# Writing the recurrence's output transposed, in two column halves, and packing it into features by SBUF transfers

## The chip, the cores and the metric

The kernel runs on one core of a Trainium2 chip. The metric is the device time in microseconds. The kernel before takes 729.41 us, the median of three runs (729.29 to 730.01). A profile of one execution, with every instruction's start and duration, is what the readings below come from.

## What is computed

A gated recurrence (4 batches, 8 heads, 768 tokens, head dimension 48), and a SwiGLU MLP (384 to 1536 to 384) on its output, with the heads side by side as 384 features of 3072 tokens:

```python
f = 1.0 / (1.0 + np.exp(-f_logit))
for t in range(S):
    state = f[:, :, t, :, None] * state + np.einsum('bhd,bhe->bhde', k[:, :, t], v[:, :, t])
    y[:, :, t] = np.einsum('bhd,bhde->bhe', q[:, :, t], state)
x = y.transpose(0, 2, 1, 3).reshape(B * S, H * D)
g = x @ w_gate
out = (g * (1.0 / (1.0 + np.exp(-g))) * (x @ w_val)) @ w_out
```

All data is float32 on the chip (the weights come as 64-bit floats and are converted there).

## The kernel before, in words

`short_path` does the work; `general_path` is a fallback that a flag selects at the end and that these inputs do not take. The tokens are cut into 6 chunks `c` of 128. A unit is one batch `b` of one chunk, so a chunk has 4 units and there are 24. The 8 heads form 4 pairs `a`; the two heads of a pair (`par` 0 and 1) lie in partition halves that begin at 0 and 64, each using 48 rows (`rows_of`, L448).

`attention(u)` (L454) is a generator that yields between steps. Step 0 transposes the gate logits of a unit on TensorE (`fTp`, L462) and applies the sigmoid on ScalarE (L467). Step 1 makes products of gates by a scan on VectorE (L472). Step 2 transposes `k` and `q` (L462), scales them (L483 to L487) and, after the first chunk, asks for the loads of the unit three ahead (`load_after`, L489) and decays the state on GpSimd (L491). Step 3 makes the scores `sc` (L499: the two heads of a pair use the two row halves of the array), masks them to `A` on VectorE (L501) and transposes `k` back (`kt`, L506). Step 4 makes the output `y` (L516 and L519), copies it to `x` (L522), and updates the state through `dS` (L526), whose heads alternate between two partition halves of the output. Step 5 transposes `x` into features by tokens (`xTp`, L542) and copies it into the chunk's `xT` (L543), which holds all 4 units, 512 tokens.

In L516 and L519 the tokens are the stationary operand (`qT` and `A`, 128 columns) and the state (96 columns for a pair) or `v` (48 columns for a head) streams, so `y` comes out with tokens in partitions.

`mlp(c)` (L558) is a list of pieces: 24 that make the hidden layer (`gate` and `val`, 12 of each, L564, each 3 matmuls over 512 tokens), then 4 `down` (L577), one for each batch, 12 matmuls each (L580), followed by a copy and a store on ScalarE's queue (L583, L585). Every `gate` and `val` streams the whole `xT` of the chunk, so the first `gate` needs all 4 units.

The order of work is set in three places. First, chunk 0's attention is written out by hand with `run(b, steps)` (L628 to L660), and `in_order` ties TensorE, VectorE and ScalarE to it, not the SP queue. Second, `mlp(c)` and the attention of chunk c+1 take turns (`take_turns`, L590): `attention_steps` (L550) groups the steps of each unit by `parts = [1, 2, 1, 1, 1]` and sorts those groups by `2 * b + s`, and step group i of n falls due after a proportional number of MLP pieces. In chunk 0 the MLP's pieces also include the calls that fetch and convert weights (`weights`, L602). Third, the framework orders each engine's and each queue's instructions by its own plan of readiness, with program order as the priority, so something that is ready earlier can pass what is not.

All loads of q, k, v and f (`load`, L378) and of weights (L399) are issued on the SP queue; only the stores of the output go through ScalarE's queue. There are 3 buffers for each of `f`, `k` and `q`, 6 for `v`, 2 for `xT` and for `x`, 4 PSUM banks for the attention (`bank`, L451) and 4 for the MLP.

Of the kernel before, what the change touches and what calls it, by code (L numbers as in the profile page):

```python
# [9 lines left out]
FP32 = mybir.dt.float32  # L10
# [279 lines left out]
def short_path(ctx, tc, least, judge, q, k, v, f_logit, moe_w_gate, moe_w_val, moe_w_out, out):  # L290
# [9 lines left out]
    nc = tc.nc  # L300
    B, H, S, D = q.shape
    C = 128
    NCH = S // C
    HP = H // 2
    W = 64
    DM = H * D
    KT = DM // 128
    DFF = moe_w_out.shape[0]
    NF = DFF // 128
    TB = B * C  # L310
# [6 lines left out]
    att = ctx.enter_context(tc.tile_pool(name="att", bufs=2))  # L317
    ffn = ctx.enter_context(tc.tile_pool(name="ffn", bufs=2))
# [5 lines left out]
    ident = const.tile([128, 128], FP32, tag="ident", name="ident")  # L324
# [12 lines left out]
    def keep_warm(n):  # L337
        p = fps.tile([128, 512], FP32, tag="m", name="idle")
        for _ in range(n):
            nc.tensor.matmul(p, lhsT=blank[:, 0:128], rhs=blank, start=True, stop=True)  # L340
# [15 lines left out]
    def pairs(t, off=0):  # L356
        return t[:, off:off + HP * N1].rearrange("p (a t) -> p a t", t=N1)
# [18 lines left out]
    vt = {}  # L376
# [69 lines left out]
    xT = {}  # L446

    def rows_of(par):  # L448
        return slice(W * par, W * par + D)

    def bank(name):  # L451
        return aps.tile([128, 512], FP32, tag="a", name=name)

    def attention(u):  # L454
        b, c = units[u]
        fr, kr, qr = (raw[nm][u % NRAW] for nm in "fkq")
        gate, tail, start = (x[u % NROT] for x in (gates, tails, starts))

        def transposed(name, src):
            p = bank(name)  # L460
            for a in range(HP):
                nc.tensor.transpose(p[:, a * C:(a + 1) * C],  # L462
                                    src[:, 2 * a:2 * a + 2, :].rearrange("t r d -> t (r d)"), ident)
            return p.rearrange("p (a t) -> p a t", t=C)

        p = transposed("fTp", fr)
        nc.scalar.activation(pairs(gate)[:, :, 1:N1], p, AF.Sigmoid)  # L467
        yield


        n = HP * N1
        nc.vector.tensor_tensor_scan(tail[:, 0:n][:, ::-1], gate[:, 0:n][:, ::-1], ones[:, ::-1], 1.0,  # L472
                                     op0=ALU.mult, op1=ALU.add)
        whole = pairs(tail)[:, :, 1:2]
        nc.vector.tensor_tensor(least, least, whole.rearrange("p a t -> p (a t)"), ALU.min)
        nc.vector.tensor_single_scalar(pairs(start)[:, :, 0:1], whole, LEAST, op=ALU.max)
        nc.vector.reciprocal(pairs(start)[:, :, 0:1], pairs(start)[:, :, 0:1])
        yield

        kp = transposed("kTp", kr)  # L480
        qp = transposed("qTp", qr)
        kT = att.tile([128, HP, C], FP32, tag="kT", name="kT")
        nc.vector.tensor_tensor(kT, kp, pairs(tail, 2)[:, :, 0:C], ALU.mult)  # L483
        head = att.tile([128, n], FP32, tag="head", name="head", bufs=1)
        nc.vector.tensor_tensor_scan(head, gate[:, 0:n], start, 1.0, op0=ALU.mult, op1=ALU.add)  # L485
        qT = att.tile([128, HP, C], FP32, tag="qT", name="qT")
        nc.vector.tensor_tensor(qT, qp, pairs(head)[:, :, 1:N1], ALU.mult)  # L487
        if c:
            load_after(u)  # L489
            decayed = att.tile([128, HP, 2, D], FP32, tag="decayed", name="decayed")  # L490
            nc.gpsimd.tensor_tensor(decayed, states[b], whole.unsqueeze(2).broadcast_to((128, HP, 2, D)), ALU.mult)  # L491
        yield

        A = att.tile([128, 2, HP, C], FP32, tag="A", name="A")
        sc = [bank("sc") for _ in range(2)]
        for a in range(HP):
            for par in range(2):
                r = rows_of(par)
                nc.tensor.matmul(sc[par][:, a * C:(a + 1) * C], lhsT=kT[r, a, :], rhs=qT[r, a, :], start=True, stop=True)  # L499
        for par in range(2):  # L500
            nc.vector.tensor_tensor(A[:, par], sc[par].rearrange("p (a t) -> p a t", t=C),  # L501
                                    causal.unsqueeze(1).broadcast_to((128, HP, C)), ALU.mult)
        if c < NCH - 1:
            p = bank("kt")
            for a in range(HP):
                nc.tensor.transpose(p[:, a * C:(a + 1) * C], kT[:, a, :], ident)  # L506
            kt = att.tile([128, H, W], FP32, tag="kt", name="kt")
            nc.scalar.copy(kt, p.rearrange("t (h d) -> t h d", d=W))
        yield


        y = bank("y")
        for a in range(HP):
            both = y[:, 2 * a * D:2 * (a + 1) * D]
            if c:
                nc.tensor.matmul(both, lhsT=qT[:, a, :], rhs=decayed[:, a, :, :].rearrange("p r d -> p (r d)"),  # L516
                                 start=True, stop=False, skip_group_check=True)
            for par in range(2):
                nc.tensor.matmul(both[:, par * D:(par + 1) * D], lhsT=A[:, par, a, :], rhs=vt[u][:, 2 * a + par, :],  # L519
                                 start=(c == 0), stop=True, skip_group_check=True)  # L520
        x = att.tile([128, DM], FP32, tag="x", name="x")
        nc.scalar.copy(x, y[:, 0:DM])  # L522
        if c < NCH - 1:
            p = bank("dS")
            for h in range(H):
                nc.tensor.matmul(p[W * (h % 2):W * (h % 2) + W, (h // 2) * D:(h // 2 + 1) * D],  # L526
                                 lhsT=kt[:, h, :], rhs=vt[u][:, h, :], start=True, stop=True)
            dS = p[:, 0:HP * D].rearrange("p (a d) -> p a d", d=D)
            for par in range(2):
                half = slice(W * par, W * par + W)  # L530
                if c:
                    nc.vector.tensor_tensor(states[b][half, :, par, :], decayed[half, :, par, :], dS[half], ALU.add)  # L532
                else:
                    nc.scalar.copy(states[b][half, :, par, :], dS[half])
        yield


        if b == 0:
            xT[c] = ffn.tile([128, KT, TB], FP32, tag="xT", name="xT", bufs=2)
        p = bank("xTp")  # L540
        for i in range(KT):
            nc.tensor.transpose(p[:, i * C:(i + 1) * C], x[:, i * 128:(i + 1) * 128], ident)  # L542
        nc.scalar.copy(xT[c][:, :, b * C:(b + 1) * C], p[:, 0:KT * C].rearrange("p (a t) -> p a t", t=C))  # L543
        yield

    def load_after(u):
        if u + NRAW < len(units):
            load(u + NRAW)

    def attention_steps(c):  # L550

        runs = [attention(c * B + b) for b in range(B)]
        parts = [1, 2, 1, 1, 1]
        order = sorted((2 * b + s, b, n) for b in range(B) for s, n in enumerate(parts))
        return [lambda b=b, n=n: [next(runs[b]) for _ in range(n)] for _, b, n in order]

# [57 lines left out]
    mark = traced[-1]  # L614
    keep_warm(5)
    first = [attention(b) for b in range(B)]
    done = [0] * B

# [9 lines left out]
    def run(b, *steps):  # L628
        for s in steps:
            assert done[b] == s  # L630
            done[b] += 1
            next(first[b])
# [5 lines left out]
    for b in range(1, B):  # L638
        if b == 1:
            run(1, 0)  # L640
            keep_warm(12)
        run(b, 1)
        run(b - 1, 3)
        run(b, 2)
        if b + 1 < B:
            run(b + 1, 0)
        else:
            sizes.pop(0)()
        run(b - 1, 4)
        if b > 1:  # L650
            run(b - 2, 5)
            load_after(b - 1)
    run(B - 1, 3)
    joins.pop(0)()
    run(B - 1, 4)
    run(B - 2, 5)
    run(B - 1, 5)
    sizes.pop(0)()
    joins.pop(0)()
    load_after(B - 1)  # L660
# [3 lines left out]
    for c in range(NCH):  # L664
        pieces = mlp(c)
        if c == 0:
            hidden, pieces = pieces[:2 * NF], pieces[2 * NF:]
            turns = [1] * NF
            for i in range(len(joins) - NF):
                turns[NF - 1 - i] += 1  # L670
            pieces = [f for i in range(NF) for f in hidden[2 * i:2 * i + 2] + [weights] * turns[i]] + pieces
        take_turns(pieces, attention_steps(c + 1) if c + 1 < NCH else [])
        if c == NCH - 2:
            judge(bank)
# [4 lines left out]
def kernel(  # L679
# [22 lines left out]
    def judge(bank):  # L702
# [9 lines left out]
                                   skip_runtime_bounds_check_because="a comparison"))  # L712

    short_path(tc, least, judge, *args)
    with tc.If(redo[0] > 0):
        general_path(tc, *args)
# [32 lines left out]
```

## Time and profile before

| | us |
|---|---|
| three runs, median | 729.41 |
| the profiled execution | 729.66 |
| its span, first to last instruction | 727.9 |
| mean granted TensorE clock | 0.998 of full speed |

Groups that the change touches, from the groups of instructions (busy time is summed over overlapping instructions):

| group | instructions | busy us | mean ns |
|---|---|---|---|
| `y` from state, L516, TensorE | 160 | 32.8 | 286 |
| `y` from `A`, L519, TensorE | 384 | 53.5 | 267 |
| `xTp`, L542, TensorE | 72 | 11.8 | 275 |
| copy `x`, L522, ScalarE | 24 | 11.5 | 478 |
| copy `xT`, L543, ScalarE | 24 | 11.4 | 479 |

The duration of a matmul in these rows includes its passage through the array; matmuls overlap, so what one costs is read from the distance between starts. An f32 matmul appears as two instructions, a transpose as one. In a timeline line the first number is the start in us from the span's beginning, the second the time that the merged instructions cover, then engine, line, operation, output and inputs, count, and in brackets idle time before it with what ended it. SPq and ACTq are the issue of transfers by those queues.

### The profile page before, as it was taken

The page shows a single profiled execution, that of the slowest core. Times are in us where ns is not written, and L with a number is a line of the kernel's source. Part 1 is how long each engine was busy: PE and PEld are TensorE (multiplying, and loading weights), DVE is VectorE, ACT ScalarE, POOL GpSimd, SP SyncE. Part 2 cuts the span into 40 slices and gives each one's busy share as a digit, 9 for nine tenths or more (in the row PEclk, how much of TensorE's full clock was granted, in tenths as well). Part 3 has the DMA queues.
Part 4 walks back from the last instruction along what each step waited for, and adds up shares of the span by engine and source line. Part 5 has one row for each costly group of instructions (what it writes and reads, how often), then busy time and mean ns, then how long its engine had stood idle before and what let it go on. Part 6 is the DMA issues. An engine that isn't in the chain of part 4 may idle for free.

```text
span 727.9 us, 7635 instructions
## 1 busy us (share of the span) xinstructions
PE 718.8 (99%) x3146; PEld 415.8 (57%) x3146; DVE 248.9 (34%) x405; ACT 185.2 (25%) x272; POOL 21.6 (3%) x43
## 2 busy tenths in 40 slices
PE   8999999999999999999999999999999999999997
PEld 6845555655555665555566555556555566544454
DVE  8799797024234003333202433311333320011100
ACT  2655473032212103323103213301223210100100
POOL 2000000000000000000000000000000000000000
PEclk9999999999999999999999999999999999999999
DMA  9988463112111002211101112010200000000000
GB/s 194 249 224 226 140 172 76 32 35 43 32 33 40 26 23 44 44 23 32 33 23 43 33 33 43 12 32 23 45 1 1 0 1 23 23 0 1 0 23 24
DMA packets 109772, 38.34 MB, mean 53 GB/s; under 512 B 100512, under 2 KB 103584, under 8 KB 109728
## 3 DMA queue, kind: packets, MB, share of 16 engines
q1 hardware_dynamic: 106272, 33.04, 19.5%
q10 hardware_dynamic: 3456, 4.72, 1.8%
q8 instruction: 27, 0.44, 0.2%
q14 instruction: 17, 0.14, 0.1%
HBM read 33.03 MB, written 4.72 MB: 52 GB/s over the span
## 4 chain that ended last, share of the span: by engine, by line
PE 97%; DVE 1%; ACT 1%; DMA 1%; SPq 0%; issue 0%; DVEq 0%
PE o L580 26%; PE val L564 26%; PE gate L564 26%; PE y L519 5%; PE sc L499 4%; PE y L516 3%; PE dS L526 2%; PE kt L506 2%; PE qTp L462 1%; PE kTp L462 1%; PE fTp L462 1%; PE xTp L542 1%; DMA fraw<-in_f_logit_dram 1%; PE idle L340 0%; ACT xT L543 0%; ACT ob L583 0%
## 5 line engine op out<-in xcount | busy, mean ns | idle before, releaser
L564 PE MATMUL gate<-xT,w_gate 128*128 128x512 f32 x432 | 196.4, 596 | 0.8 <-ACT xT L543 0.5
L564 PE MATMUL val<-xT,w_val 128*128 128x512 f32 x432 | 195.7, 595 | 0.1
L580 PE MATMUL o<-w_out,h 128*128 128x384 f32 x576 | 188.8, 487 | 0.0
L580 PEld LDWEIGHTS o<-w_out,h 128*128 128x128 f32 x576 | 108.3, 190 | 73.2 <-issue 0.5
L564 PEld LDWEIGHTS val<-xT,w_val 128*128 128x128 f32 x432 | 79.1, 190 | 86.5 <-issue 84.9
L564 PEld LDWEIGHTS gate<-xT,w_gate 128*128 128x128 f32 x432 | 78.5, 190 | 84.4 <-issue 81.8
L575 DVE TENSOR_TENSOR h<-h,val 128x512 f32<-128x512 f32 x72 | 49.2, 684 | 184.0 <-PE val L564 184.0
L571 ACT ACTIVATE h<-gate 128x512 f32<-128x512 f32 x72 | 42.9, 597 | 205.6 <-PE gate L564 205.4
L472 DVE TENSOR_TENSOR_SCAN tails<-gates,ones 128x516 f32<-128x516 f32 x24 | 29.5, 1231 | 91.5 <-ACT gates L467 91.5
L501 DVE TENSOR_TENSOR A<-sc,causal 128x512 f32<-128x512 f32 x48 | 30.9, 684 | 81.2 <-PE sc L499 81.2
L583 ACT COPY ob<-o 128x384 f32<-128x384 f32 x24 | 11.5, 478 | 183.5 <-PE o L580 183.5
L519 PE MATMUL y<-v,A 128*128 128x48 f32 x384 | 53.5, 267 | 0.4 <-issue 0.2
L519 PEld LDWEIGHTS y<-v,A 128*128 128x128 f32 x384 | 49.7, 192 | 0.8 <-issue 0.4
L491 POOL TENSOR_TENSOR decayed<-state,tails 128x384 f32<-128x384 f32 x20 | 17.4, 868 | 561.8 <-DVE tails L472 561.8
L485 DVE TENSOR_TENSOR_SCAN head<-gates,starts 128x516 f32<-128x516 f32 x24 | 33.4, 1391 | 0.6
L516 PE MATMUL y<-decayed,qT 128*128 128x96 f32 x160 | 32.8, 286 | 0.0
L499 PEld LDWEIGHTS sc<-qT,kT 48*128 48x128 f32 x384 | 23.6, 187 | 15.3 <-issue 13.6
L516 PEld LDWEIGHTS y<-decayed,qT 128*128 128x128 f32 x160 | 25.8, 192 | 8.5 <-issue 6.9
L467 ACT ACT_TABLE_LOAD x20 | 25.7, 1283 | 16.1 <-PE fTp L462 13.5
L499 PE MATMUL sc<-qT,kT 48*128 48x128 f32 x384 | 28.4, 285 | 0.0
L532 DVE TENSOR_TENSOR state<-decayed,dS 64x192 f32<-64x192 f32 x32 | 11.2, 351 | 48.2 <-PE dS L526 47.9
L571 ACT ACT_TABLE_LOAD x20 | 25.7, 1283 | 0.4
(58 smaller groups left out, 350.3 us busy)
## 6 DMA issues: line engine op xcount, KB each, us to landing
fraw<-in_f_logit_dram SPq DMA_DIRECT2D x24, 192.0 KB, 3.1
kraw<-in_k_dram SPq DMA_DIRECT2D x24, 192.0 KB, 3.0
qraw<-in_q_dram SPq DMA_DIRECT2D x24, 192.0 KB, 3.5
v<-in_v_dram SPq DMA_DIRECT2D x24, 192.0 KB, 3.5
w<-in_moe_w_gate_dram SPq DMA_DIRECT2D x6, 768.0 KB, 6.2
w<-in_moe_w_val_dram SPq DMA_DIRECT2D x6, 768.0 KB, 5.9
w<-in_moe_w_out_dram SPq DMA_DIRECT2D x6, 768.0 KB, 4.4
out_dram<-ob ACTq DMA_DIRECT2D x24, 192.0 KB, 1.8
```

The source lines that it names most:

```text
L462: nc.tensor.transpose(p[:, a * C:(a + 1) * C], src[:, 2 * a:2 * a + 2, :].rearrange("t r d -> t (r d)"), ident)
L467: nc.scalar.activation(pairs(gate)[:, :, 1:N1], p, AF.Sigmoid)
L472: nc.vector.tensor_tensor_scan(tail[:, 0:n][:, ::-1], gate[:, 0:n][:, ::-1], ones[:, ::-1], 1.0, op0=ALU.mult, op1=ALU.add)
L485: nc.vector.tensor_tensor_scan(head, gate[:, 0:n], start, 1.0, op0=ALU.mult, op1=ALU.add)
L499: nc.tensor.matmul(sc[par][:, a * C:(a + 1) * C], lhsT=kT[r, a, :], rhs=qT[r, a, :], start=True, stop=True)
L501: nc.vector.tensor_tensor(A[:, par], sc[par].rearrange("p (a t) -> p a t", t=C), causal.unsqueeze(1).broadcast_to((128, HP, C)), ALU.mult)
L516: nc.tensor.matmul(both, lhsT=qT[:, a, :], rhs=decayed[:, a, :, :].rearrange("p r d -> p (r d)"), start=True, stop=False, skip_group_check ...
L519: nc.tensor.matmul(both[:, par * D:(par + 1) * D], lhsT=A[:, par, a, :], rhs=vt[u][:, 2 * a + par, :], start=(c == 0), stop=True, skip_gro ...
L564: nc.tensor.matmul(p, lhsT=w[:, i, j * 128:(j + 1) * 128], rhs=xT[c][:, i, :], start=(i == 0), stop=(i == KT - 1))
L571: nc.scalar.activation(h[j], p, AF.Silu)
L575: nc.vector.tensor_tensor(h[j], h[j], p, ALU.mult)
L580: nc.tensor.matmul(p, lhsT=h[j][:, b * C:(b + 1) * C], rhs=w_out[:, j, :], start=(j == 0), stop=(j == NF - 1))
```

## The change

`y` is written with features in partitions: `v` (48 columns for a head) and the decayed state (48 columns for a head) are now loaded, and the tokens (`A` and `qT`, 128 columns) stream. The heads of a pair write two partition halves of one PSUM bank (0 to 47 and 64 to 111), and pair `a` writes columns 128a to 128a+127. Two ScalarE copies, one for each half, bring it to `x`. Then transfers issued on the SP queue move rows of `x` to the rows of `xT` at which their features belong: one transfer for a head, two for a head whose 48 features cross a multiple of 128 (heads 2 and 5), 10 for each unit. The transpose step is gone, so `parts` has one entry less and the hand-written start has no step 5.

```diff
+        if b == 0:
+            xT[c] = ffn.tile([128, KT, TB], FP32, tag="xT", name="xT", bufs=2)
         y = bank("y")
         for a in range(HP):
-            both = y[:, 2 * a * D:2 * (a + 1) * D]
+            cols = slice(a * C, (a + 1) * C)
             if c:
-                nc.tensor.matmul(both, lhsT=qT[:, a, :], rhs=decayed[:, a, :, :].rearrange("p r d -> p (r d)"),
-                                 start=True, stop=False, skip_group_check=True)
+                for par in range(2):
+                    nc.tensor.matmul(y[rows_of(par), cols], lhsT=decayed[:, a, par, :], rhs=qT[:, a, :],
+                                     start=True, stop=False, skip_group_check=True)
             for par in range(2):
-                nc.tensor.matmul(both[:, par * D:(par + 1) * D], lhsT=A[:, par, a, :], rhs=vt[u][:, 2 * a + par, :],
+                nc.tensor.matmul(y[rows_of(par), cols], lhsT=vt[u][:, 2 * a + par, :], rhs=A[:, par, a, :],
                                  start=(c == 0), stop=True, skip_group_check=True)
-        x = att.tile([128, DM], FP32, tag="x", name="x")
-        nc.scalar.copy(x, y[:, 0:DM])
+        x = att.tile([128, HP, C], FP32, tag="x", name="x")
+        for par in range(2):
+            nc.scalar.copy(x[rows_of(par)], y[rows_of(par)].rearrange("p (a t) -> p a t", t=C))
+
+        for h in range(H):
+            f = h * D
+            while f < (h + 1) * D:
+                n = min((h + 1) * D, (f // 128 + 1) * 128) - f
+                r = W * (h % 2) + f - h * D
+                nc.sync.dma_start(out=xT[c][f % 128:f % 128 + n, f // 128, b * C:(b + 1) * C],
+                                  in_=x[r:r + n, h // 2, :])
+                f += n
...
-        if b == 0:
-            xT[c] = ffn.tile([128, KT, TB], FP32, tag="xT", name="xT", bufs=2)
-        p = bank("xTp")
-        for i in range(KT):
-            nc.tensor.transpose(p[:, i * C:(i + 1) * C], x[:, i * 128:(i + 1) * 128], ident)
-        nc.scalar.copy(xT[c][:, :, b * C:(b + 1) * C], p[:, 0:KT * C].rearrange("p (a t) -> p a t", t=C))
-        yield
...
-        parts = [1, 2, 1, 1, 1]
+        parts = [1, 2, 1, 1]
...
         if b > 1:
-            run(b - 2, 5)
             load_after(b - 1)
...
     run(B - 1, 4)
-    run(B - 2, 5)
-    run(B - 1, 5)
```

## The prediction

> **What bounds the kernel now.** I read the busy shares first, then the slices, then the chain that ended last.
>
> ```profile
> PE 718.8 (99%) x3146; PEld 415.8 (57%) x3146; DVE 248.9 (34%) x405; ACT 185.2 (25%) x272; POOL 21.6 (3%) x43
> ...
> PE   8999999999999999999999999999999999999997
> ...
> DMA  9988463112111002211101112010200000000000
> ...
> PE 97%; DVE 1%; ACT 1%; DMA 1%; SPq 0%; issue 0%; DVEq 0%
> ```
>
> TensorE is the chain nearly everywhere: time removed there is gained and every hole made there is paid. Only in the first two slices (36 us) are the DMA engines and VectorE full as well. A timeline of one steady unit shows what its matmuls cost, and one of the last chunk boundary what stands between a chunk's last `y` and the next MLP's first `gate`:
>
> ```profile
> 167.97 1.16 PE L499 MATMUL sc<-qT,kT 48*128 48x128 f32 x16
> ...
> 177.09 0.43 PE L516 MATMUL y<-decayed,qT 128*128 128x96 f32 x2
> ...
> 177.35 0.57 PE L519 MATMUL y<-v,A 128*128 128x48 f32 x4
> 177.85 0.55 PEld L526 LDWEIGHTS dS<-v,kt 128*64 128x64 f32 x16
> 177.85 0.67 PE L526 MATMUL dS<-v,kt 128*64 128x48 f32 x16
> 177.96 0.48 ACT L522 COPY x<-y 128x384 f32<-128x384 f32 x1 [3.12 <-PE y L519]
> ```
>
> ```profile
> 620.48 0.57 PE L519 MATMUL y<-v,A 128*128 128x48 f32 x4
> ...
> 620.88 7.97 PE L580 MATMUL o<-w_out,h 128*128 128x384 f32 x24
> ...
> 628.69 0.49 PE L542 MATMUL xTp<-ident,x 128*128 128x128 f32 x3
> ...
> 629.27 0.48 ACT L543 COPY xT<-xTp 128x384 f32<-128x384 f32 x1
> ...
> 629.80 2.41 PE L564 MATMUL gate<-xT,w_gate 128*128 128x512 f32 x5 [0.51 <-ACT xT L543]
> ```
>
> See in the first: an f32 matmul is two instructions; six of them (two of L516, four of L519) take 0.67 us, 112 ns each, although they stream only 96 or 48 columns. `dS`, whose outputs alternate between partition halves 0 and 64, does 16 in 0.60 us. In the second: the last unit's `y` is followed by a whole `down` (7.9 us) before its transpose, so `gate` waits only 0.8 us.
>
> **What the skill says.** "TensorE: Matmul & The Clock Gate", section "LDWEIGHTS", prices a weight load at columns / 1.2 ns: 107 ns for 128 columns, 40 for 48. The trace agrees: `y` paced at 112 by loads of 128 columns. The same page, "Part 3: Packing small matmuls — row/col tiling", says that matmuls in different column groups run together. The trace agrees: single records of `dS` start in pairs 6 ns apart, a pair each 58 ns; those of `sc` (row halves, 128 columns streamed) a pair each 112 ns. "TensorEngine Tiling (Array Packing)", "Key Properties", says that a change of tiling mode drains the array: from the last `y` record to the first `dS` is 205 ns instead of 112, some 0.09 us for the change.
>
> **The change, part by part.**
>
> *Matmuls of `y`.* Now, chunks 1 to 5: first `y` record to first `dS` 2.70 us per unit; in chunk 0 (no state term) 1.81. Then: per pair `a`, two state and two `A` matmuls of two instructions, 8, so 32 per unit, halves alternating. Streaming 128 columns as `sc` does, with 48-column loads underneath, gives 16 pairs x 0.112 = 1.79 us; chunk 0, 8 pairs, 0.90. The mode change moves ahead of `y` (+0.09); chunk 5, with no `dS` to share it, pays both ends (+0.19). Saved: 0.82 per unit in chunks 1 to 4, 0.63 in chunk 5, 0.82 in chunk 0. No row shows full rows with 128 columns in two column halves. The bounds are 1.79 (the halves run together) and 32 x 0.112 = 3.58 (they don't). I take 1.79, as `dS` shows halves with all rows.
>
> *Transposes `xTp`.* Three instructions, 187.16 to 187.48: 0.33 us per unit gone from TensorE.
>
> TensorE sum: 16 x 1.15 + 4 x 0.96 = **-22.2 us** in chunks 1 to 5. Chunk 0's four units would give 4.6, but there VectorE sets the pace (units 5.4 us apart, its scans, products and masks near 6 us per unit), and what follows waits on transfers anyway: I count 0.
>
> *ScalarE.* Before, two copies of 0.48. Then two copies of 512 columns each (the `kt` copy of that width took 0.59): 1.2 us in a row, before the first half-1 head can be sent.
>
> *The packing.* Per unit 10 transfers on SP (heads 2 and 5 cross a border of 128 features), 240 in all, each behind the `x` copies, and `gate` behind all of them. Prices:
>
> ```profile
> 162.48 0.37 SPq L382 DMA_DIRECT2D kraw<-in_k_dram  x1
> ...
> 162.94 0.53 SPq L382 DMA_DIRECT2D qraw<-in_q_dram  x1
> ```
>
> ```profile
> fraw<-in_f_logit_dram SPq DMA_DIRECT2D x24, 192.0 KB, 3.1
> ...
> out_dram<-ob ACTq DMA_DIRECT2D x24, 192.0 KB, 1.8
> ```
>
> Two issues in a row start 0.46 us apart; a landing takes 1.8 to 3.1 us. No row shows an SBUF to SBUF transfer of 24 KB. "DMA: Bandwidth & Descriptors", "Anatomy of one DMA", gives about 2 us fixed; I take 1.8, the store's row (bounds 1.4 and 3.1). From the end of `y`: copies 1.25, nine issues after the second copy (the last begins at 1.35 + 8 x 0.44 = 4.9), landing 6.7, with one load among them about **7 us** (bounds 5.8 and 9). For the first three units of a chunk it is hidden: many microseconds of MLP lie behind. For the fourth it is not, because its cover goes too. With `parts` of four steps a chunk has 16 steps over 28 MLP pieces, and the last step falls due after piece 28, the last `down`; before, with 20 steps, `y` of unit 3 fell after piece 27 and only the transpose after 28. The trace follows these positions (`y` between the last two `down`s), so now all of `down` comes ahead of the last `y`, and nothing but the next attention is left to hide the packing.
>
> *Boundaries into chunks 1 to 4.* After `y`, TensorE has `dS` (to +0.5 us) and what the framework's own ordering brings forward: in the trace `fTp` and one `kTp` of the next unit came ahead of `gate`, which the program has after it. At most some five groups of four transposes (0.44 each, 2.2 us) have inputs and banks; `sc` of that unit lies behind sigmoid, two scans and two products (over 6 us). TensorE is done at 2.7 and `gate` begins at 7: 4.3 us idle against nearly none. 4 x 4.3 = **+17** (bounds 12 and 24).
>
> *Boundary into chunk 5.* No attention is left: idle 7 less the 0.8 of before, **+6** (5 to 8).
>
> *Into chunk 0.* SP issues without a pause until 38 us, and the transfers ahead hold it up:
>
> ```profile
> 31.80 0.84 SPq L382 DMA_DIRECT2D qraw<-in_q_dram  x1
> 32.69 0.80 SPq L384 DMA_DIRECT2D v<-in_v_dram  x1
> 33.60 0.64 SPq L399 DMA_DIRECT2D w<-in_moe_w_val_dram  x1
> ```
>
> Thirty issues of packs 0 to 2 (13 us) join this queue, part of it inside time in which SP stood blocked (issues of 0.7 to 3.1 us, some 10 us over the floor). Pack 3, with `x` ready near 32, begins near 37, takes 5 and lands near 45; `gate` began at 33.9. Less one more microsecond of brought-forward transposes: **+10** (bounds 4: nothing ahead of it delayed; 18: all 13 us added).
>
> *Smaller terms.* Weight fetches of chunk 0 queue behind packs of chunk 1 (each 4.4 us of SP), and `gate` and `val` already waited for `w_val` twice: +2 (0 to 6). Waits for many transfers at `gate`: +1. The clock: the first page named, "Part 1: The HAM clock gate", says that an idle window of about 3.4 us halves it, and a busy one of that length restores it. The trace has only the start: the first five `idle` matmuls run at 0.43 us, the twelve at 7.9 us at 0.22. A cold stretch of 4 us costs 2. Three of the six holes: +6 (0 to 12).
>
> **Sum:** -22.2 + 17 + 6 + 10 + 2 + 1 + 6 = +19.8 us on the profiled execution's 729.66 (span 727.9 and 1.8 around it), which stands 0.25 above the median of 729.41. I take **748**.
>
> **Rivals.** (A) Slower by the boundary holes, as above: 735 to 760, 0.66. (B) The holes are small: packs land in 5.8 us, the clock never drops, chunk 0 loses only 4. Then -22 + 12 + 5 + 4 = -1, and with a cheaper issue (0.3 us, for 48 rows instead of 1024 runs) about -6: 724 to 729. This is the faster side: one mechanism, the packing of the fourth unit, which decides at about 5.5 us from `y` to landing. For it: issue costs were seen only on larger transfers. Against it: an issue on ACT with an eighth of the runs was hardly shorter (0.34). 0.12. (C) The column halves don't run together: `y` 3.58, TensorE gains 0.33 - 0.88 - 0.09 = -0.6 per unit, a loss of 13 where I have 22 gained: near 780. Against it stands `dS`. 0.08. (D) The SP queue becomes the bound in chunk 0: with packs among loads and weights the first MLP starves again and again, 15 to 25 us more: near 768. For it: DMA slices 9 9 8 8. Against: 40 packs of 196 KB are under an eighth more descriptors. 0.14.
>
> **Numbers.** Differences under 0.2% (1.5 us) can't be told from no change. Faster 0.09 (most of B), same 0.04, slower 0.87. The range of 8 in 10 takes A and most of D, and leaves out B's faster part and C: 730 to 773.
>
> **What would show it.** Right: `y` at about 1.8 us per unit with records in pairs; `gate` waiting for transfers of `xT`, 4 us at boundaries 1 to 4 and some 6 at the last; no `down` between the last `y` and `gate`; the first `gate` after 40 us. Wrong: `y` records 112 ns apart singly (C); packs landed within 5 us of `y` (B); a long list of `gate` and `val` waits for weights (D); or attention of the next chunk filling the holes entirely.

## The result, and the profile after

The changed kernel takes 751.5 us, the median of four runs (751.0 to 752.14), against 729.52 before: a ratio of 1.0301, interval 1.0283 to 1.0319, so 3% slower. The forecast was 748. The profiled execution took 751.0, its span is 749.0. First the busy shares and slices of the profile after:

```profile
PE 707.3 (94%) x3234; PEld 389.7 (52%) x3234; DVE 247.5 (33%) x405; ACT 189.5 (25%) x270; POOL 21.5 (3%) x43
...
PE   8659999898999998999999899999999999799997
...
PEclk9769999898999999999999999999999999899999
DMA  9449567102022111121210211210200000000000
```

TensorE's busy time is 11.5 us less and the span 21.1 us more. Busy time hides part of it, since matmuls on the slow clock count longer (8 in 6.2 us where 16 fit at full clock, shown below): see the slices in which the granted clock falls to 7, 6 or 8 tenths. And where before the DMA engines were full for the first two slices (9 9), they now fall to 4 and 4 in the second and third: the start doesn't lack bandwidth, it lacks issued transfers.

The last unit of chunk 1 and the boundary behind it, from the timeline (the transfers in the last lines are the packs):

```profile
170.82 0.39 PE L519 MATMUL y<-qT,decayed 128*48 128x128 f32 x4
...
171.03 0.39 PE L522 MATMUL y<-A,v 128*48 128x128 f32 x4
...
171.25 0.62 PE L539 MATMUL dS<-v,kt 128*64 128x48 f32 x16
171.47 1.19 ACT L526 COPY x<-y 48x512 f32<-48x512 f32 x2 [1.42 <-PE y L522]
171.80 0.66 PE L462 MATMUL fTp<-ident,fraw 128*128 128x128 f32 x4
...
172.30 0.60 PE L462 MATMUL kTp<-ident,kraw 128*128 128x128 f32 x4
172.37 5.79 SPq L533 DMA_DIRECT2D xT<-x  x8
...
172.73 0.63 PE L462 MATMUL qTp<-ident,qraw 128*128 128x128 f32 x4
...
176.32 2.05 PE L568 MATMUL gate<-xT,w_gate 128*128 128x512 f32 x2 [2.96 <-DMA xT<-x]
```

Four `y` instructions take 0.22 us (170.82 to 171.03), two pairs of 0.11: the column halves run together, and a unit's `y`, from 169.47 to 171.25, takes 1.78 us. Then `dS`, three groups of transposes brought forward, and a hole of 2.96 us. No `down` stands between `y` and `gate`. Note that `gate` begins while SP still issues packs: it did not wait for all of them. The trace has the third of the ten landing at 176.19 us, the last at 180.65.

The SP queue in the start, from the timeline of that queue alone:

```profile
15.91 0.49 SPq L399 DMA_DIRECT2D w<-in_moe_w_gate_dram  x1
16.50 16.49 SPq L533 DMA_DIRECT2D xT<-x  x20
33.09 0.53 SPq L382 DMA_DIRECT2D fraw<-in_f_logit_dram  x1
...
36.38 6.36 SPq L533 DMA_DIRECT2D xT<-x  x10
42.84 0.53 SPq L382 DMA_DIRECT2D fraw<-in_f_logit_dram  x1
...
45.52 7.36 SPq L533 DMA_DIRECT2D xT<-x  x10
52.98 0.53 SPq L382 DMA_DIRECT2D fraw<-in_f_logit_dram  x1
```

Ten issues fill 6.3 us, 0.63 each, and loads of chunk 1 stand between the packs. The first `gate` begins at 53.11; before it was at 33.91.

**Where the time went.** I cut both traces at the first `gate` of each chunk. Lengths in us:

| | to the first `gate` | chunk 0 | 1 | 2 | 3 | 4 | 5 and end | span |
|---|---|---|---|---|---|---|---|---|
| before | 33.9 | 120.2 | 120.0 | 120.0 | 120.0 | 115.6 | 98.1 | 727.9 |
| the change | 53.1 | 123.2 | 120.3 | 117.6 | 118.6 | 114.2 | 102.0 | 749.0 |
| no packing | 32.0 | 119.8 | 115.0 | 115.0 | 115.0 | 112.1 | 98.0 | 706.9 |
| fifth step | 53.5 | 118.6 | 114.9 | 114.9 | 114.9 | 111.6 | 97.9 | 726.3 |
| chunk 0 as before | 34.3 | 126.5 | 118.8 | 119.2 | 118.6 | 114.3 | 101.8 | 733.4 |
| both | 37.1 | 117.7 | 114.9 | 114.9 | 114.9 | 111.6 | 97.7 | 708.7 |

The start loses 19.2 us; all that follows together loses 1.9, in which a gain of 19 (what the kernel without packing saves there) and a loss of 21 are hidden. The last four rows are experiments.

### The profile page after: what moved, and what is told of

The parts are those of the page before. It is cut to its first block, busy times and chain, and to the rows that moved or that the text cites. A ratio compares the mean times of both kernels' runs of the same rounds, so it can differ in the third digit from the quotient of the medians.

```text
span 749.0 us, 8178 instructions
## 1 busy us (share of the span) xinstructions
PE 707.3 (94%) x3234; PEld 389.7 (52%) x3234; DVE 247.5 (33%) x405; ACT 189.5 (25%) x270; POOL 21.5 (3%) x43
## 4 chain that ended last, share of the span: by engine, by line
PE 77%; DVE 3%; ACT 2%; DMA 1%; issue 1%; SPq 1%; ACTq 0%
PE o L584 24%; PE gate L568 22%; PE val L568 21%; PE sc L499 2%; PE y L519 2%; PE y L522 2%; DMA xT<-x 1%; PE kt L506 1%; SPq L533 1%; DVE top L419 1%; DVE w_out L420 1%; PE fTp L462 1%; PE kTp L462 1%; PE qTp L462 1%; ACT x L526 1%
## 5 line engine op out<-in xcount | busy, mean ns | idle before, releaser
L568 PE MATMUL gate<-xT,w_gate 128*128 128x512 f32 x432 | 203.1, 613 | 13.5 <-DMA xT<-x 13.5
L584 PE MATMUL o<-w_out,h 128*128 128x384 f32 x576 | 191.6, 492 | 3.6 <-DVE w_out L420 3.6
L568 PEld LDWEIGHTS gate<-xT,w_gate 128*128 128x128 f32 x432 | 81.3, 195 | 109.5 <-issue 105.6
L587 ACT COPY ob<-o 128x384 f32<-128x384 f32 x24 | 11.5, 478 | 195.1 <-PE o L584 195.1
L526 ACT COPY x<-y 48x512 f32<-48x512 f32 x48 | 27.8, 579 | 52.9 <-PE y L522 33.2
L522 PE MATMUL y<-A,v 128*48 128x128 f32 x384 | 37.0, 281 | 0.0
L483 DVE TENSOR_TENSOR kT<-kTp,tails 128x512 f32<-128x512 f32 x24 | 16.5, 686 | 51.1 <-PE kTp L462 50.9
L519 PE MATMUL y<-qT,decayed 128*48 128x128 f32 x320 | 32.6, 281 | 0.0
L485 DVE TENSOR_TENSOR_SCAN head<-gates,starts 128x516 f32<-128x516 f32 x24 | 31.5, 1311 | 0.7
L519 PEld LDWEIGHTS y<-qT,decayed 128*48 128x48 f32 x320 | 18.3, 124 | 13.7 <-issue 7.6
```

Source lines behind the costliest of these rows:

```text
L519: nc.tensor.matmul(y[rows_of(par), cols], lhsT=decayed[:, a, par, :], rhs=qT[:, a, :], start=True, stop=False, skip_group_check=True)
L522: nc.tensor.matmul(y[rows_of(par), cols], lhsT=vt[u][:, 2 * a + par, :], rhs=A[:, par, a, :], start=(c == 0), stop=True, skip_group_check= ...
L526: nc.scalar.copy(x[rows_of(par)], y[rows_of(par)].rearrange("p (a t) -> p a t", t=C))
L568: nc.tensor.matmul(p, lhsT=w[:, i, j * 128:(j + 1) * 128], rhs=xT[c][:, i, :], start=(i == 0), stop=(i == KT - 1))
L584: nc.tensor.matmul(p, lhsT=h[j][:, b * C:(b + 1) * C], rhs=w_out[:, j, :], start=(j == 0), stop=(j == NF - 1))
```

## The experiments

In the kernels without packing and with two transfers, `xT` is two fixed buffers, cleared once. My theory was the forecast's: TensorE gains some 22 us, and more than that is lost in two places, at the boundaries (the last unit's packs lost their cover) and in the start (packs on a full SP queue). Rivals were a cost of the column halves themselves, packs that are late wherever they stand, one shared cause for both losses, and, within the start, order against the time of issue.

**The matmuls without the packing.**

```diff
-        x = att.tile([128, HP, C], FP32, tag="x", name="x")
         for par in range(2):
-            nc.scalar.copy(x[rows_of(par)], y[rows_of(par)].rearrange("p (a t) -> p a t", t=C))
+            nc.scalar.copy(xT[c][rows_of(par), :, b * C:(b + 1) * C],
+                           y[rows_of(par), 0:KT * C].rearrange("p (a t) -> p a t", t=C))
...
-                nc.sync.dma_start(out=xT[c][f % 128:f % 128 + n, f // 128, b * C:(b + 1) * C],
-                                  in_=x[r:r + n, h // 2, :])
```

> Part alone: the transposed matmuls, with no packing. ScalarE copies three of the four pairs straight into rows 0 to 47 and 64 to 111 of the three feature tiles, so the fourth pair is left out and the features stand in wrong rows. Theory (TensorE gains what the forecast said, all losses come from the packing): TensorE saves 1.15 us in each of 20 units, so 729.5 - 22 to - 26: 703 to 709, first gate near 33 us, no gaps at the boundaries over 1.5 us. Rival (the column halves or the copies cost something that the gaps hide): above 718.

Measured 709.44 us (before, on the same chip, 729.74), ratio 0.9726 (0.9709 to 0.9742), 0.4 above the range expected. The span is 21.0 us shorter: 5.0 in each of chunks 1, 2 and 3, 3.5 in chunk 4, 1.9 in the start. Chunk 0 gains only 0.4, because TensorE, now early, waits for the converted `w_out` and then runs 3.4 us at half its clock:

```profile
119.71 0.96 DVE L420 CUSTOM_DVE_ANT_0 w_out<-top,up 128x1536 uint16<-128x1536 uint16 x1
...
120.72 2.51 PE L578 MATMUL o<-w_out,h 128*128 128x384 f32 x4 [2.55 <-DVE w_out L420]
```

So neither the column halves nor the copies hide a cost that eats the gain. The change without its packing would be worth 2.7%, and what turns it into a loss is the packing.

**A fifth, empty step.**

```diff
                     nc.scalar.copy(states[b][half, :, par, :], dS[half])
         yield
 
+        yield
+
...
-        parts = [1, 2, 1, 1]
+        parts = [1, 2, 1, 1, 1]
```

> The change with an empty fifth step for every unit, so that the last y of a chunk again falls due before the last down; the packing is as in the change. Theory (the boundary holes come from the step that went, whose place let the last down cover the packing): the five holes of 1.8 to 4.3 us and the cold clock behind three of them go, some 18 to 22 us, so 730 to 735; the start stays as it is, first gate near 53. Rival (the packing itself is too long or too late wherever y stands): within 5 us of 751.

Measured 728.14 us against 729.74, ratio 0.998 (0.9964 to 0.9997), a little less than the 730 to 735 expected. That is 23 us less than the change, from two lines that compute nothing. The timeline of the boundary into chunk 3 (`o` is the last `down`):

```profile
394.63 6.25 SPq L533 DMA_DIRECT2D xT<-x  x10
394.81 7.26 PE L586 MATMUL o<-w_out,h 128*128 128x384 f32 x22
401.90 1.45 PE L570 MATMUL gate<-xT,w_gate 128*128 128x512 f32 x3
```

The same ten issues, 6.25 us long, now lie under the last `down`, and `gate` waits for nothing. Chunks 1 to 5 have the lengths of the kernel without packing; the start is as long as in the change. With the same transfers, issued the same way, the boundary losses are gone: they come from the place of the step.

**The clock in the holes.**

```diff
         pieces = mlp(c)
+        if c:
+            keep_warm(10)
```

> The change with ten bf16 matmuls on a blank tile (2.2 us) ahead of each chunk's first gate from chunk 1 on, in the holes while the packs land; nothing else changed. Theory (behind three of the holes TensorE runs on at half its clock, 3.4 to 6.8 us each time): the cold stretches at 176, 414 and 647 us go, the holes keep their length, 751.5 - 8 = 742 to 746. Rival (the cold clock only lies where TensorE would have waited anyway): within 2 us of 751.5.

Measured 743.04 us, ratio 1.0177 (1.0153 to 1.02), against 1.0301: 9 us less, by matmuls on a blank tile. In the change, the clock records show half clock for 6.8 us at 176, 3.4 at 414 and 6.8 at 647, worth half of that, 8.5, at most: 1.6 us of these stretches lie in the holes themselves. The windows 176.3 to 182.5 and the next 6.2 us show it by TensorE alone: 8 matmuls in the first, 16 in the second.

```profile
176.30:182.50 6.20, 6.18 (x8) 2.59 (x9) 2.55 (x4) 0.00 (x0) 0.54 (x1) 0.50 0.35 74
182.50:188.70 6.20, 6.20 (x16) 2.82 (x15) 0.69 (x1) 1.19 (x2) 0.00 (x0) 1.00 0.22 44
```

Columns are the window, its length, busy time and count of TensorE, weight loads, VectorE, ScalarE and GpSimd, then granted clock, DMA share and GB/s. With the blank matmuls none of these stretches is in the records; chunk 1 is 2.9 us shorter than in the change, chunk 3 1.7, the end 3.6, chunks 2 and 4 0.5 and 0.9 longer (there `gate` waits longer for transfers: it comes 5.10 us after the last `y` of chunk 2, not 4.58, and waits 0.72 a second time in chunk 4). The remaining 2.0 us are in chunk 0, where no cold stretch followed the wait for `w_out`, equally long (2.44 us), though no matmul was put there; they are not shown to be the edit's (the last section has what decides on such a stretch).

**Chunk 0 as before.**

```diff
+        if not c:
+            y = bank("y")
+            for h in range(H):
+                nc.tensor.matmul(y[:, h * D:(h + 1) * D], lhsT=A[:, h % 2, h // 2, :], rhs=vt[u][:, h, :],
+                                 start=True, stop=True, skip_group_check=True)
+            x = att.tile([128, DM], FP32, tag="x", name="x")
+            nc.scalar.copy(x, y[:, 0:DM])
+        else:
...
+        if not c:
+            p = bank("xTp")
...
```

> The change in chunks 1 to 5 alone; chunk 0 writes y and transposes as before, so 40 of the 240 transfers go. Theory (the start loses its 19 us to the packs of chunk 0 on the SP queue, and the wait for w_out later in chunk 0 is their echo): first gate near 34, 751.5 less 19 to 27: 724 to 732. Rival (the loss is given back by later packs among weights and loads): above 738.

Measured 735.47 us, ratio 1.0083 (1.0066 to 1.01). The first `gate` comes at 34.3, so the start's loss is all back; but the time lies between my two cases. Chunk 0 grew to 126.5 us: its waits for `w_out` (4.5 us) did not go, and the hole at its end (3.4) stayed. That the waits for `w_out` were an echo of the start has fallen; the kernel without packing has one too. There TensorE reaches its first `down` 7.1 us earlier than before the change (111.6 against 118.6) and the last piece of `w_out` is converted only 3.1 us earlier (120.7 against 123.8). Here, with packs among the fetches, TensorE is 4.6 us earlier than before the change and `w_out` 3.2 later, so an earlier TensorE is the larger part and late weights are the rest.

**Order or issue time.** Chunk 0's packs move behind the loads of a later unit:

```diff
...
+        if not c:
+            pack()
+            yield
...
             load_after(b - 1)
+            run(b - 2, 5)
```

> The change with chunk 0's packs issued one unit later, each behind the loads of a later unit, so the loads of units 4, 5 and 6 no longer queue behind two packs each; the number of transfers is the same. Theory 1 (what counts is the order: loads stand behind packs that wait for x, the DMA engines run empty): first gate 8 us or more earlier, 738 to 744. Theory 2 (what counts is the time that SP needs to issue 40 transfers at 0.6 us): the last pack is out no earlier, first gate within 4 us of 53, time within 5 us of 751.5.

Measured 753.28 us, ratio 1.0306 (1.028 to 1.0332), the first `gate` at 58.3. Theory 1 has fallen; theory 2 has the time right, but the first `gate` is 5.2 us later than in the change, not within 4. The SP queue of this kernel:

```profile
25.54 1.20 SPq L384 DMA_DIRECT2D v<-in_v_dram  x1
26.83 6.29 SPq L534 DMA_DIRECT2D xT<-x  x10
33.23 0.53 SPq L382 DMA_DIRECT2D fraw<-in_f_logit_dram  x1
...
36.33 6.48 SPq L534 DMA_DIRECT2D xT<-x  x10
...
46.60 14.24 SPq L534 DMA_DIRECT2D xT<-x  x20
```

The loads of unit 4 are early, yet each ten issues fill 6.3 to 7 us as before, and the last pack goes out at 60. Here `gate` does wait for packs, 4.04 us. What is put first only decides what comes last.

**A fifth of the issues.**

```diff
-        for h in range(H):
...
+        for par in range(2):
+            nc.sync.dma_start(out=xT[c][rows_of(par), :, b * C:(b + 1) * C], in_=x[rows_of(par), 0:KT, :])
```

> The change with two transfers for each unit instead of ten, each of one half and three pairs; the fourth pair is left out and the features stand in wrong rows. Three quarters of the bytes move by a fifth of the issues, and y stays behind the last down. Theory (SP's time for the issues sets the start, 0.63 us each): first gate at 34 to 38; holes at the boundaries still there, since copies and a landing of 1.8 us remain, 1 to 3 us each with cold stretches behind some: 726 to 735. Rival (what costs is that SP waits for x and holds up what is behind it, however few the transfers): first gate above 45, time above 742.

Measured 731.71 us (before, on this chip, 731.04), ratio 1.0008 (0.9989 to 1.0027). The first `gate` comes at 35.5, with the packs on the same queue, behind the same `x`. So the number of issues is what the start pays. The holes at the boundaries are hardly shorter, 1.7 to 3.9 us, and the last is longer than expected: two copies and one landing (2.4 us, for 72 KB) are enough to make them.

**The packs on another queue.**

```diff
-                nc.sync.dma_start(out=xT[c][f % 128:f % 128 + n, f // 128, b * C:(b + 1) * C],
+                nc.gpsimd.dma_start(out=xT[c][f % 128:f % 128 + n, f // 128, b * C:(b + 1) * C],
```

> The change with the packs issued on GpSimd's queue instead of SP's; order of steps and number of transfers unchanged. Theory (SP's issue time and order cost the start): loads and weights go out as before the change, first gate 36 to 45, and the later waits for w_out go; boundaries as in the change or longer if GpSimd issues more slowly: 733 to 745. Rival (the transfers themselves slow the others wherever they are issued): first gate above 50, time at or above 751.

Measured 745.06 us, ratio 1.0192 (1.0171 to 1.0212). The first `gate` is at 40.7, 12 us earlier than in the change, with the same 40 transfers. Part of the loss stays, since GpSimd too issues one by one:

```profile
15.49 4.12 POOL L533 DMA_DIRECT2D xT<-x  x8 [10.62 <-ACT x L526]
...
27.42 11.65 POOL L533 DMA_DIRECT2D xT<-x  x22 [0.46 <-DMA xT<-x]
```

That is 0.51 to 0.53 us an issue, and the last pack goes out at 40. The holes at the boundaries are 2.9 to 3.8 us. A wait of 2.04 us for `w_out` is still there, which the theory had going.

**Both places mended.** Chunk 0 as before, with the fifth step:

> Chunk 0 as before the change, and the change in chunks 1 to 5 with the empty fifth step. Theory (the loss is two separate things, the start and the boundaries): the two gains add, 751.5 - 16 - 23 = 712, within 3 us of the 709.4 of the kernel without packing; first gate near 34, no gap over 1 us at a boundary. Rival (they share a cause, late packs on a full SP queue): the gains overlap, above 718.

Measured 710.3 us (706.58 to 712.23) against 731.04, ratio 0.9715 (0.9691 to 0.9739), the first `gate` at 37.1. That is 2.8 us later than with chunk 0 as before alone, because in this execution the twelve blank matmuls of the start ran at half clock, 5.25 us in place of 2.75. The two gains add: the change is at 1.0301, the step takes 0.032 off, the start 0.022, which makes 0.976, and 0.9715 was measured. This version beats both kernels, and its chunks 1 to 5 are as long as those of the kernel without packing: transfers that lie under a `down` cost nothing measurable.

```profile
PE 698.1 (99%) x3246; PEld 388.7 (55%) x3246; DVE 247.5 (35%) x405; ACT 190.6 (27%) x272; POOL 21.6 (3%) x43
...
PE   8999999899999999999999999999999999999997
...
PEclk9999999999999999999999999999999999999999
```

TensorE is full again and its clock whole. What remains, one gap of 2.7 us for `w_out` at 127.6 us, is in chunk 0.

## Why the prediction was right, and where its terms were off

The direction and the main mechanism were right, and 748 against 751.5 lies inside the range (the sum as written gives 749.2). That the size is so close is luck: the boundaries were put 10 us too high (17 and 6 against 9.2 and 3.8), the start 9 too low.

- **`y` and `xTp` on TensorE: right.** 1.78 us a unit against 1.79, 0.91 in chunk 0 (13.69 to 14.60) against 0.90, pairs as `dS` had shown. The sum, -22.2, came out as -21.0 without packing. Within it more errors offset one another: the attention of chunk 0, counted at 0, gave 1.9 in the start; that of chunk 1, counted at 4.6, gave only 0.4, the rest lost to the wait for `w_out` and the slow clock behind it; that of the other four chunks, counted at 17.6, gave 18.6.
- **The cover of the fourth unit: right in mechanism, too large in size.** I had 4.3 us idle at each of four boundaries, 17 in all; the holes are 2.96, 2.10, 2.36 and 1.79, 9.2 in all. The step that failed is "`gate` behind all of them". A `gate` is three matmuls over three feature tiles, and the first of them needs its own tile alone, three of ten transfers. At each of the five boundaries `gate` begins 0.1 to 0.4 us after the third of the ten landed, and the last lands 4.1 to 4.4 us after `gate` has begun. The whole packing was longer than I had, 8.2 to 9.4 us from `y` to the last landing and not 7, since an issue took 0.63 and not 0.44; this works the other way.
- **The boundary into chunk 5: nearly right.** A hole of 3.63 and a second of 0.65, less the 0.5 of before: +3.8 against +6, for the same reason.
- **The start: too small, and outside its own bounds.** I had +10 (4 to 18); it is +19.2. The step that failed is "Thirty issues of packs 0 to 2 (13 us) join this queue, part of it inside time in which SP stood blocked". 40 issues at 0.63 are 25 us, not 18, and little was absorbed. From 16.5 to 53.0 us SP spent 27 us on packs, 6 on the eight loads between them and 3.1 waiting for weight transfers. I had taken the distance from a first issue to a second, 0.46; the row shown beside it, the second issue's own 0.53, is nearer to what a run of issues costs. Rival D named this queue, but placed the loss in the first MLP's waits for weights; most of it fell ahead of the first `gate`. There is a second loop that I did not see: with two buffers for `x`, ScalarE's copies of units 2 and 3 waited 2.94 and 3.69 us for packs of units 0 and 1. What more buffers would give was not tested.
- **The clock: right in kind, +6 against about +8** at the boundaries. The Trainium skill ("TensorE: Matmul & The Clock Gate", "Part 1: The HAM clock gate") gives half clock after an idle window of some 3.4 us; here the records show it behind idle stretches of only 2.4 to 3.6 us, at three of five boundaries, for 3.4 or 6.8 us, so the measurement decides. There are two stretches of 10.2 us more in the start and one of 6.8 behind the wait for `w_out`.
- **Weights, +2:** 0.76 for `w_val` and 3.6 for `w_out`, but packs ahead of fetches, the reason given, are not the main one: without any packs the wait for `w_out` is there, 2.55 us.
- **Rivals.** B's holes, 12 and 5, were nearer than mine to the 9.2 and 3.8 measured; it failed on the start (4 against 19.2) and on the clock (nothing against about 8). C failed on the pairs. The sign named for "right", 4 us of waiting at boundaries 1 to 4 and 6 at the last, did not come: it was 1.8 to 3.0 and 3.6.

Left open: how much of the start is lost through late loads of chunk 1 and how much through the last pack. In the change's own trace it is the late loads that end last. TensorE waits for chunk 1's `fraw`, then for its `qT`, and does that attention ahead of the first `gate`; `gate` itself then waits for no pack, since the three that its first tile needs had landed by 49.3:

```profile
35.96 1.11 PE L462 MATMUL fTp<-ident,fraw 128*128 128x128 f32 x4 [4.14 <-DMA fraw<-in_f_logit_dram]
...
47.58 2.08 PE L499 MATMUL sc<-qT,kT 48*128 48x128 f32 x16 [8.39 <-DVE qT L487]
...
53.11 1.12 PE L568 MATMUL gate<-xT,w_gate 128*128 128x512 f32 x2
```

With the loads put first the packs end last, so order can't win the start back; and the two-transfer kernel, which shortens both, can't part them.

## What to carry to other kernels

A step that is removed also moves what stays: here one empty step for each unit was worth 23 us, since it decided whether the last unit's transfers lay under a matmul block or in front of one. Before trusting a hidden transfer, ask of the last unit of each stage what still runs behind it, and count issues, not bytes: many small transfers on one queue cost that queue's time one by one, and a queue that is free later may be the bound at the start. Where consumers read a buffer in parts, price the wait for the part that they need first.

## What the runs showed of the hardware

- A run of small issues costs SP 0.63 us each (0.59 and a gap), the same for 16, 32 or 48 rows of 512 bytes, and no less than a load of 1024 runs in a row of loads (0.62). GpSimd's queue takes 0.51 to 0.53.
- An SBUF to SBUF transfer of 8 to 24 KB lands in 1.7 to 1.8 us on the median from its issue on SP (1.7 at least, 8.0 at most).
- The length of a hole alone does not decide whether TensorE's clock falls. In each of the ten traces all changes of the granted clock lie whole steps of 3413 ns apart, to within 2 ns. Cut a trace into windows at these steps: behind the first `gate`, half clock followed each of the 33 windows in full clock that had 1.97 us or more without a matmul, and none of the others, which had 1.95 or less (in the start, with its small matmuls, 1.70 was enough; the ends of matmuls are modelled, so these bounds hold for these traces). So a hole of 2.66 us that fell on two windows, 1.32 and 1.34, left the clock whole (the kernel with both places mended, at 124.92), and one of 2.02, nearly all in one window, did not (two transfers, at 276.40). Likewise the wait of 2.44 for `w_out` lies in one window in the change and is split 1.71 and 0.73 in the kernel with the blank matmuls. The stretch behind the hole of 2.66, with the granted clock, 1.00, as the third number from the end, and then the one behind the hole of 2.02, at 0.50:

```profile
127.58:131.00 3.42, 3.42 (x11) 2.09 (x12) 0.00 (x0) 0.48 (x1) 0.00 (x0) 1.00 0.13 48
```

```profile
279.86:283.27 3.41, 3.41 (x6) 1.35 (x5) 2.02 (x4) 0.60 (x1) 0.01 (x1) 0.50 0.35 71
```

- Column halves with all 128 rows and 128 columns streamed run in pairs, a pair each 0.11 us, as row halves do.
